# A second X table buffer, generators in two batches, spectra in three slots and a new stage order in a two-branch kernel

## The chip, the cores and the metric

The kernel runs on one core of a Trainium2 chip. The metric is device time in microseconds of one execution, the median of the runs shown; less is better.

## The reference

Two branches of the same 2048 positions by 640 channels stand side by side in the output (2048 by 1280, bf16).

```
A: q, k, v = heads(x @ wqkv)                     # 32 heads of 20
   logits[s, w] = q[s] . k[s - 2 w] * 20**-0.5   # w = 0..7, masked before 0
   out_A = (softmax(logits) @ v[s - 2 w]) @ wo
B: K[d, l] = Re sum_n C dt B exp(dt A l)         # 192 complex terms, l = 0..2047
   out_B = causal convolution of u with K, as FFTs of length 4096, + u * Dskip
```

## The kernel before

Branch B works in five chunks of channels (`NCH`, 192 terms wide in the free dimension, with the 128 channels of a chunk on the partitions). For each chunk `K` is a contraction of two tables over the terms, X (20 exponents) and Y (33 exponents), so that each product of entries is one power of `exp(dt A)`. Generators are the powers at exponents 2**0 to 2**10: `magnitudes` (L234) makes their absolute values on ScalarE, `gens` (L245 to L258) their sines and cosines: a shift and an absolute value on VectorE, two sines on ScalarE and one product on VectorE for each power. Chunk 0's generators go straight into its tables; those of chunk 1 (`gens1`) and of chunks 2 to 4 (`gens2`) go to DRAM (`Gd`, L671) and are loaded by `Tables.load` (L289). `ymag` makes the 16 magnitudes that `yneg` (L315) needs for Y's negative exponents, `ypos` the positive ones, `xtab` X by complex products (`cmul`, L270 to L275) from `Gt` of `weights` or `Xg[:, 6]`; its first product takes `Y[:, 32]`. `kgen` (L345 to L362) contracts both tables with 512 small matmuls a chunk. X, Xg and Y have one buffer each.

The rest of branch B for a chunk: `first_u` and `spread`/`f1` make the first FFT stage of u and K, `f2` the spectra (L410, copied by ScalarE at L414), `swap_halves` a copy of u's spectrum with its halves swapped, `product` (L424, L425) the product of the spectra, `ia` the first inverse stage (L437), stored as `Zd` for chunks 0 to 2 and kept as `Z34` for 3 and 4. Eight pieces `last00` to `last13` (`inverse`, L797) end it: each loads u (`uq`, L804), multiplies it by Dskip (L806), adds it to matmuls with the constant `HB` (L813), copies to `ysb` (L814) and stores (L816); `last0*` also load `zq` from `Zd` (L821). HB takes the space of the tables once the last contraction is done.

Branch A: `proj` makes q, k and v for 5 column tiles each (L473, L474) and stores them; four blocks of 512 positions then run `fetch`, `fetch_v`, `logits` (L522, L526), `av` (L552, L558) and `out_proj` (L571).

The order of the work is not that of the text. Every stage stands in `with at(name)`, which gives its instructions the rank of its name in the list `ORDER` as priority; a planner fills each engine's and queue's instruction stream by these priorities, by dependencies and by free buffers. The streams are fixed after that, and each engine and each queue (SP's, which issues nearly all transfers, POOL's, ScalarE's) goes through its own in order. `pin` adds an order of its own among the activations that need different function tables.

Of the kernel before, what the change touches and what calls it, by code (L numbers as in the profile page):

```python
# [147 lines left out]
def partB_prep(tc, pools, prm, Gd):  # L148
# [53 lines left out]
    def weights():  # L202
# [4 lines left out]
        Gt = pp.tile([128, NCH, 2, CW], bf16, name="Gt")  # L207
        br, bi = flip(4, True), flip(5, True)
        pr = [pp.tile([128, Wd], f32, name=f"pr{q}") for q in range(2)]
        for c0, c1, r in ((0, 1, 0), (1, 0, 1)):  # L210
            for (s, b0), (_, b1) in zip(br, bi):
                V.tensor_tensor(out=pr[0][:, s], in0=b0, in1=cc[:, c0, s], op=A.mult)
                if r == 0:
                    V.tensor_tensor(out=pr[1][:, s], in0=b1, in1=cc[:, c1, s], op=A.mult)
                else:
                    V.scalar_tensor_tensor(out=pr[1][:, s], in0=b1, scalar=-1.0, in1=cc[:, c1, s], op0=A.mult, op1=A.mult)
            p3 = [pr[q][:].rearrange("p (c n) -> p c n", c=NCH) for q in range(2)]
            if r == 0:
                V.tensor_tensor(out=Gt[:, :, 0], in0=p3[0], in1=p3[1], op=A.subtract)
            else:  # L220
                V.tensor_tensor(out=Gt[:, :, 1], in0=p3[1], in1=p3[0], op=A.subtract)
        nc.sync.dma_start(out=Gd[1:, :, 6].rearrange("c p r n -> p c (r n)"), in_=Gt[:, 1:].rearrange("p c r n -> p c (r n)"))
# [7 lines left out]
def magnitudes(tc, pools, ta, am, ca, cb):  # L230

    s = slice(CW * ca, CW * cb)
    for k in K_ORDER:
# [630 lines left out]
```

## Time and profile before

| what | us |
|---|---|
| median of 3 runs | 503.28 (502.35 to 505.78) |
| profiled execution | 505.62 |
| its span, first to last instruction | 503.5 |
| TensorE busy in it | 347.2 |
| VectorE busy | 311.3 |
| ScalarE busy | 265.0 |

The span is what the rows of the trace cover; the 2.1 us around it are not in them. Busy time adds up the instructions of one engine; engines overlap, and idle time counts only where the engine is the one that the end waits for. A window is a stretch of the span for which the busy time of each engine is given, with the mean TensorE clock granted in it (1.00 is 2.4 GHz).

### The profile page before, as it was taken

The numbers are of one execution on the slowest core, as the hardware profiler recorded it, in microseconds if no ns is written. First come the engines' busy times: TensorE is split into PE (matmuls) and PEld (weight loads), VectorE is DVE, ScalarE is ACT, GpSimd is POOL, SyncE is SP. The second block draws the span as 40 slices with busy tenths as digits, with TensorE's granted clock in tenths as the row PEclk, the third lists the DMA queues.
The fourth block names the chain that finished last, engine by engine and source line by source line (L and its number), as shares of the span: only waits on it lengthen the run. The fifth ranks groups of instructions, "written<-read, shape, count | busy, mean of one in ns | idle before, by whom it ended". The sixth has DMA issues, their size and how long they took to land.

```text
span 503.5 us, 13288 instructions
## 1 busy us (share of the span) xinstructions
PE 347.2 (69%) x5684; PEld 215.4 (43%) x5684; DVE 311.3 (62%) x479; ACT 265.0 (53%) x592; POOL 36.4 (7%) x80
## 2 busy tenths in 40 slices
PE   0584298779698728899687596666397788764633
PEld 0232045434246214468444364434165566563422
DVE  0688896599860798987079995189991383021110
ACT  1769866467441164796066652167252587841211
POOL 6820000300000200000020000100000100000000
PEclk9999599599797666899668688599788699775656
DMA  8998684565550577637441029331017650408554
GB/s 251 179 146 182 164 230 155 172 212 204 190 187 5 158 215 203 149 97 206 148 112 23 22 64 279 99 100 23 23 40 199 231 194 33 107 27 226 148 104 70
DMA packets 87562, 70.20 MB, mean 139 GB/s; under 512 B 42864, under 2 KB 79328, under 8 KB 86480
## 3 DMA queue, kind: packets, MB, share of 16 engines
q1 hardware_dynamic: 84096, 63.93, 46.7%
q0 software_dynamic: 2352, 5.18, 3.8%
q8 instruction: 44, 0.72, 0.6%
q10 hardware_dynamic: 1056, 0.25, 0.2%
q14 instruction: 14, 0.11, 0.1%
HBM read 37.35 MB, written 23.63 MB: 121 GB/s over the span
## 4 chain that ended last, share of the span: by engine, by line
PE 34%; DVE 20%; DMA 13%; ACT 10%; issue 8%; SPq 2%; POOL 0%; DVEq 0%; ACTq 0%; POOLq 0%
PE ps_p L473 7%; PE ps_op L571 5%; DVE p L552 4%; PE ps_k L357 4%; PE ps_ia L437 4%; PE ps_k L352 4%; DMA Gdram<-cs 4%; DMA uq<-Udram 3%; DVE krtmp L271 3%; ACT A L396 3%; DVE prod L522 2%; ACT Sp L414 2%; DMA Ytab<-Gdram 2%; PE ps_l L526 2%; DMA qb<-qd 2%
## 5 line engine op out<-in xcount | busy, mean ns | idle before, releaser
L473 PE MATMUL ps_p<-xT,w 128*128 128x512 bf16 x300 | 82.9, 431 | 23.7 <-ACT st L474 18.3
L473 PEld LDWEIGHTS <-w 128*128 128x128 bf16 x300 | 31.1, 107 | 70.2 <-issue 43.6
L522 DVE TENSOR_TENSOR prod<-qb,kb 128x2048 bf16<-128x2048 bf16 x40 | 47.7, 1219 | 15.9 <-DMA kb<-kd 10.9
L558 PE MATMUL ps_o<-p,cHs 64*32 64x256 bf16 x640 | 36.4, 310 | 24.9 <-DVE p L552 23.1
L474 ACT CAST st<-ps_p 128x512 bf16<-128x512 f32 x60 | 34.2, 583 | 34.4 <-PE ps_p L473 32.5
L396 ACT CAST A<-ps_f 128x512 bf16<-128x512 f32 x80 | 42.4, 610 | 18.2 <-PE ps_f L395 18.1
L414 ACT CAST Sp<-ps_f 128x512 bf16<-128x512 f32 (+1 forms) x96 | 42.4, 555 | 16.6 <-PE ps_f L410 16.5
L552 DVE TENSOR_TENSOR p<-vb,attn 128x2048 bf16<-128x2048 bf16 x40 | 48.0, 1218 | 1.9 <-PE ps_o L558 1.8
L357 PE MATMUL ps_k<-Ytab,Xtab 64*20 64x33 bf16 x1280 | 28.0, 244 | 22.8 <-issue 22.8
L410 PE MATMUL ps_f<-A,cT 64*128 64x128 bf16 (+1 forms) x768 | 34.2, 227 | 13.5 <-DMA cT<-k_T 10.3
L270 DVE TENSOR_TENSOR Ytab<-Ytab 128x384 bf16<-128x384 bf16 (+2 forms) x15 | 13.3, 886 | 42.9 <-DMA Ytab<-Gdram 42.8
L410 PEld LDWEIGHTS <-cT 64*128 64x128 bf16 x768 | 27.8, 105 | 26.2 <-issue 14.5
L359 ACT CAST Kd<-ps_k 128x264 bf16<-128x264 f32 x20 | 7.5, 377 | 58.5 <-PE ps_k L357 58.5
L806 DVE TENSOR_TENSOR uq<-uq,Dsb 128x1536 bf16<-128x1536 bf16 (+1 forms) x8 | 6.6, 825 | 46.0 <-DMA uq<-Udram 38.9
L357 PEld LDWEIGHTS <-Xtab 64*20 64x20 bf16 x1280 | 22.4, 123 | 27.1 <-issue 25.0
L558 PEld LDWEIGHTS <-cHs 64*32 64x32 bf16 x640 | 16.0, 99 | 37.1 <-issue 25.4
L814 ACT CAST ysb<-ps_ib 128x384 bf16<-128x384 f32 (+1 forms) x24 | 11.3, 523 | 38.2 <-DMA out_dram<-ysb 25.6
L526 PE MATMUL ps_l<-prod,cGs 128*32 128x512 bf16 x160 | 25.3, 426 | 6.5 <-DVE prod L522 6.4
L571 PE MATMUL ps_op<-wo,oT 128*128 128x320 bf16 x160 | 27.9, 324 | 1.9 <-ACT oT L562 1.9
L352 PE MATMUL ps_k<-Ytab,Xtab 128*20 128x33 bf16 x1280 | 26.9, 249 | 2.4 <-issue 2.4
L424 DVE TENSOR_TENSOR UT<-Sp,UT 128x2048 bf16<-128x2048 bf16 x10 | 11.9, 1220 | 21.8 <-ACT Sp L414 21.8
L438 ACT CAST Z<-ps_ia 128x512 bf16<-128x512 f32 x40 | 20.9, 600 | 8.4 <-PE ps_ia L437 8.2
(108 smaller groups left out, 636.5 us busy)
## 6 DMA issues: line engine op xcount, KB each, us to landing
vb<-vd SPq DMA_DIRECT2D x80, 65.5 KB, 2.3
UT<-Sp SPq DMA_DIRECT2D x10, 512.0 KB, 6.6
HB<-k_HB SPq DMA_DIRECT2D x4, 1024.0 KB, 9.6
Gdram<-cs SPq DMA_DIRECT2D x11, 288.0 KB, 3.6
Zdram<-Z SPq DMA_DIRECT2D x3, 1024.0 KB, 9.2
zq<-Zdram SPq DMA_DIRECT2D x12, 256.0 KB, 4.0
Xg<-Gdram SPq DMA_DIRECT2D x4, 672.0 KB, 6.1
kb<-kd SPq DMA_DIRECT2D x4, 657.5 KB, 8.5
```

Source lines behind the costliest of these rows:

```text
L352: MM(o, lhsT=X[:, :, part, col], rhs=Y[:, :, part, col], start=False, stop=False, tile_position=(0, 32 * g), skip_group_check=True)
L357: MM(o, lhsT=X[hb:hb + 64, :, part - 2, col], rhs=Y[hb:hb + 64, :, part - 2, col], start=False, stop=(part == 3), tile_position=(hb, 32 * ...
L396: nc.scalar.copy(out=A1[:].rearrange("p k r s t -> p (k r) s t")[:, :, sig, 8 * q:8 * q + 8], in_=ps[:])
L410: nc.tensor.matmul(ps[h][:, kk], lhsT=C["T"][hs, k, 64 * (1 - r):64 * (1 - r) + 128], rhs=A1[hs, k, r, s0:s1, :].rearrange("p s t -> p (s ...
L414: nc.scalar.copy(out=o, in_=ps[h][:].rearrange("p k x -> p x k"))
L473: nc.tensor.matmul(ps[:], lhsT=self.w[which][:, kt, 128 * ct:128 * ct + 128], rhs=self.xT[:, kt, 512 * sc:512 * sc + 512], start=(kt == 0) ...
L474: nc.scalar.copy(out=st[:, sc], in_=ps[:])
L522: V.tensor_tensor(out=pr[:], in0=q[:, ct].unsqueeze(1).to_broadcast([128, 4, PB]), in1=windows(k[:, ct, 8 - 8 * wg:8 - 8 * wg + PB], 2, 4) ...
L526: nc.tensor.matmul(ps[mp][r:r + 32], lhsT=C["Gs"][:, ct, :], rhs=pr[:, 2 * mp:2 * mp + 2, PH * half:PH * half + PH], start=(ct == 0), stop ...
L552: V.tensor_tensor(out=p2[:], in0=windows(self.v[b][t][:, 2 * qp:2 * qp + 2, 0:PH], 2, 4), in1=at[:].unsqueeze(2).to_broadcast([128, 4, 2, ...
L558: nc.tensor.matmul(ps[half][32 * q:32 * q + 32, t % 2], lhsT=C["Hs"][r], rhs=p2[r, m, q2, :], start=(t % 2 == 0 and m == 0), stop=(m == 3) ...
L571: nc.tensor.matmul(ps[:], lhsT=oT[:, t, 128 * s:128 * s + 128], rhs=self.wo_sb[:, t, 320 * eh:320 * eh + 320], start=(t == 0), stop=(t == 4))
```

## The change

X gets two buffers (`bufs=2`), and Xg an eighth slot with the generator of 2**7, which `xtab` uses instead of `Y[:, 32]`. Loads of X's and of Y's generators are stages of their own (`tab*`, `taby*`), and so are the magnitudes (`mag*`). Generators are made in two batches, chunks 0 and 1, then 2 to 4; both go through DRAM, the first stored by ScalarE's queue. `cs` gets four buffers. `weights` goes by halves, with `nat` in five buffers. The spectra lie in one tile of three slots: slot 0 for K and the product, 1 and 2 in turn for u. `fetch` loads q and k in ten parts; the products of `logits` and `av` share three buffers. `uq` and `ysb` get two. ORDER is new. The core of the diff:

```diff
-G_SLOTS = [1, 2, 4, 256, 512, 1024, None, 8, 16, 32, 64, 128]
+G_SLOTS = [1, 2, 4, 256, 512, 1024, None, 128, 8, 16, 32, 64]
...
-prep mag0 yneg0 kgen0 q2 mag1 gens1 k3 weights k1 tab1 ypos0 kgen1 u0 q0 q4 xtab1 v2 ypos1 gens0 v1 fetchv0 xtab2 v4 prod0 k4 xtab0 k2 v0
-load kgen4 yneg1 load2 q3 spec swap1 u1 kgen3 spread0 spec0 u v3 prod3 inv0 xtab4 logits0 swap0 inv1 ypos2 fetch1 yneg2 spec1 out1 spread1
-yneg3 inv3 spec2 gens2 hb out0 swap4 k0 av0 swap2 last13 ypos3 swap3 last12 kgen2 xtab3 tab4 fetch2 spread3 tab2 yneg4 ypos4 u2 logits1
-spread2 last03 fetchv1 tab3 fetchv3 last01 av1 last11 q1 logits2 inv2 u3 fetch0 spec3 u4 prod2 last02 prod1 out2 av2 spread4 av3 last00
-fetch3 fetchv2 out3 last10 logits3 inv4 prod4 spec4
+k4 am2 inv4 v0 weights k0 u1 spec2 am0 q3 tab2 tab4 v3 prep load taby2 ypos1 ypos0 out1 xtab2 xtab0 tab1 tab0 q2 q1 swap1 k1 yneg1 load2 v2
+mag2 u0 yneg0 fetch0 v4 q0 spread0 k2 tab3 mag0 kgen2 mag1 gens0 kgen4 last13 q4 fetch1 spec1 inv0 kgen1 kgen0 u2 ypos2 gens2 v1 prod4 taby3
+yneg2 kgen3 k3 taby4 spec3 spec0 taby1 fetch2 ypos3 yneg4 spread3 inv3 logits0 swap0 xtab1 last10 xtab3 u3 inv2 spread1 taby0 u av3 av0
+fetchv0 swap2 last12 av2 out0 prod1 inv1 yneg3 prod2 logits3 spec xtab4 mag4 last03 u4 fetchv1 ypos4 last11 last02 last01 swap3 mag3 out3
+fetchv3 prod3 spec4 fetchv2 spread2 fetch3 av1 swap4 spread4 prod0 last00 out2 logits1 logits2 hb
...
+                pr = [pp.tile([128, 512], f32, name="pr", tag="pr", bufs=2)[:, 0:s.stop - s.start] for _ in range(2)]
+                V.tensor_tensor(out=pr[1], in0=b1, in1=cc[:, c1, s], op=A.mult)
+                    V.tensor_tensor(out=Gt[:, 0, s], in0=pr[0], in1=pr[1], op=A.subtract)
+                    V.scalar_tensor_tensor(out=Gt[:, 1, s], in0=pr[0], scalar=-1.0, in1=pr[1], op0=A.mult, op1=A.subtract)
...
-            cs = gp.tile([128, 4, 2, CW], bf16, name="cs", tag="cs", bufs=2)[:, 0:n]
+        cs = gp.tile([128, 3, 2, CW], bf16, name="cs", tag="cs", bufs=4)[:, 0:n]
+        (nc.sync if ca else nc.scalar).dma_start(out=Gd[ca:cb, :, G_SLOTS.index(2 ** k)].rearrange("c p r n -> p c (r n)"), in_=cs.rearrange("p c r n -> p c (r n)"))
...
-        self.X = tp.tile([128, 20, 2, CW], bf16, name="Xtab", tag="Xtab")
-        self.Xg = tp.tile([128, 7, 2, CW], bf16, name="Xg", tag="Xg")
+        self.X = tp.tile([128, 20, 2, CW], bf16, name="Xtab", tag="Xtab", bufs=2)
+        self.Xg = tp.tile([128, 8, 2, CW], bf16, name="Xg", tag="Xg")
+    def loadx(self, Gd):
+        if self.c:
+            self.nc.sync.dma_start(out=self.Xg[:], in_=Gd[self.c, :, 0:8])
+        else:
+            self.nc.sync.dma_start(out=self.Xg[:, 7:8], in_=Gd[0, :, 7:8])
+            self.nc.sync.dma_start(out=self.Xg[:, 0:6], in_=Gd[0, :, 0:6])
+    def loady(self, Gd):
         for k in range(5):
+            self.nc.sync.dma_start(out=self.Y[:, 16 + 2 ** k], in_=Gd[self.c, :, 8 + k if k < 4 else 7])
...
-        self.mg = [self.pools["prep" if early else "tab"].tile([128, 8, CW], bf16, name="mag", tag="mag", bufs=4 if early else 1) for _ in range(2)]
+        self.mg = [self.pools["tab"].tile([128, 8, CW], bf16, name="mag", tag="mag", bufs=2) for _ in range(2)]
...
-        cmul(nc, X[:, 0:1], Xg[:, 6:7] if w is None else w, self.Y[:, 32], tmp[:, 0:1], True)
+        cmul(nc, X[:, 0:1], Xg[:, 6:7] if w is None else w, Xg[:, 7], tmp[:, 0:1], True)
...
+            o = Sp[:, slots, h, :, 4 * q:4 * q + 4]
+            nc.scalar.copy(out=o, in_=ps[h][:].rearrange("p k (s t) -> p s t k", t=64))
+        nc.vector.tensor_tensor(out=UT[:, h], in0=SK[:, h], in1=UT[:, h], op=A.mult)
+        nc.vector.tensor_tensor(out=SK[:, h], in0=SK[:, h], in1=SU[:, h], op=A.mult)
...
+        for ct in range(5):
+            q = p.tile([128, PB], bf16, name="qb", tag="qb", bufs=3)
+            k = p.tile([128, HALO + PB], bf16, name="kb", tag="kb", bufs=3)
+            nc.sync.dma_start(out=q[:], in_=self.qd[:, ct, i0:i0 + PB])
+            nc.sync.dma_start(out=k[:], in_=self.kd[:, ct, i0:i0 + PB + HALO])
...
-                pr = p.tile([128, 4, PB], bf16, name="prod", tag="prod", bufs=2)
+                pr = p.tile([128, 4, PB], bf16, name="prod", tag="pr", bufs=3)
-                p2 = p.tile([128, 4, 2, PH], bf16, name="p2", tag="p2", bufs=2)
+                p2 = p.tile([128, 4, 2, PH], bf16, name="p2", tag="pr", bufs=3)
...
+    tabs = {}
+        am = pp.tile([128, 11, 3 * CW], bf16, name="am", tag="am")[:, :, 0:(cb - ca) * CW]
+        with at(f"am{ca}"):
+            magnitudes(tc, pools, ta, am, ca, cb)
+        with at(f"gens{ca}"):
+            gens(tc, pools, wi, am, ca, cb, Gd)
+        with at(f"xtab{c}"):
+            tabs[c].xtab(w)
+    batch(0, 2)
+    def table(c, p):
+        tabs[c] = Tables(tc, pools, c)
+        with at(f"tab{c}"):
+            tabs[c].loadx(Gd)
+        with at(f"taby{c}"):
+            tabs[c].loady(Gd)
+        with at(f"mag{c}"):
+            tabs[c].ymag(ta, p)
+    table(0, pin)
+    table(1, pin)
+    batch(2, 5)
+    with at("gens2"):
+        pin(nc.scalar.preload_act_table_set("natural_log_exp_and_others"))
+    Kds[0] = make(0, Gt[:, :, 0:CW].unsqueeze(1))
...
+    Sp = fp.tile([128, 3, 2, 64, 32], bf16, name="Sp")
-        f2(tc, pools, C, A1, SU, 1, 2)
+        f2(tc, pools, C, A1, Sp, 1, 2, slice(1, 2))
...
-            f2(tc, pools, C, A1, Sp, 0, 1 if last else 2)
+            f2(tc, pools, C, A1, Sp, 0, 1 if last else 2, slice(0, 1) if last else slice(0, 3 - c % 2, 2 - c % 2))
-            product(nc, Sp, SU, UT)
+            product(nc, Sp[:, 0], Sp[:, 1 + c % 2], UT)
...
-        uq = ip.tile([128, 6 * 256], bf16, name="uq", tag="uq", bufs=1)[:, 0:512 * n].rearrange("p (x l t) -> p x l t", x=2 * n, l=16)
+        uq = ip.tile([128, 6 * 256], bf16, name="uq", tag="uq", bufs=2)[:, 0:512 * n].rearrange("p (x l t) -> p x l t", x=2 * n, l=16)
-        ysb = ip.tile([128, 16 * 96], bf16, name="ysb", tag="ysb", bufs=1)[:, 0:512 * n].rearrange("p (l x) -> p l x", l=16)
+        ysb = ip.tile([128, 16 * 96], bf16, name="ysb", tag="ysb", bufs=2)[:, 0:512 * n].rearrange("p (l x) -> p l x", l=16)
```

## Rows read from the trace of the kernel before

**Rows 1.** Section 1 of the page, busy us (share of the span) and instructions of each engine

```profile
PE 347.2 (69%) x5684; PEld 215.4 (43%) x5684; DVE 311.3 (62%) x479; ACT 265.0 (53%) x592; POOL 36.4 (7%) x80
```

**Rows 2.** Windows of the whole core: stretch, length, busy us of each engine, TensorE clock, DMA share

```profile
core 0: us, PE busy (x) PEld busy (x) DVE busy (x) ACT busy (x) POOL busy (x), PEclk, DMA share, GB/s
0.00:81.60 81.60, 45.49 (x239) 19.67 (x239) 57.05 (x138) 53.93 (x135) 20.55 (x41) 0.90 0.85 197
...
150.60:165.00 14.40, 12.03 (x514) 9.48 (x509) 1.34 (x1) 1.82 (x5) 0.95 (x3) 0.74 0.06 17
165.00:235.80 70.80, 52.51 (x688) 31.70 (x690) 65.01 (x82) 44.58 (x106) 2.26 (x11) 0.79 0.62 171
235.80:252.00 16.20, 11.53 (x518) 9.51 (x518) 0.29 (x1) 2.42 (x7) 0.19 (x1) 0.72 0.58 159
252.00:305.30 53.30, 41.82 (x508) 24.16 (x507) 49.58 (x68) 34.09 (x77) 2.49 (x6) 0.77 0.26 69
305.30:326.00 20.70, 11.04 (x516) 9.54 (x516) 5.97 (x5) 2.40 (x6) 0.45 (x2) 0.64 0.64 180
326.00:379.60 53.60, 36.25 (x502) 21.63 (x500) 49.49 (x68) 31.04 (x68) 2.21 (x4) 0.88 0.20 51
...
395.30:448.80 53.50, 43.40 (x708) 33.86 (x709) 23.19 (x20) 42.66 (x96) 2.21 (x4) 0.83 0.38 122
448.80:503.50 54.70, 25.55 (x284) 18.75 (x281) 5.64 (x7) 12.03 (x26) 0.00 (x0) 0.61 0.57 132
```

**Rows 3.** Windows of the instructions that write or read Xtab, VectorE, one stretch

```profile
252.00:305.30 53.30, 15.13 (x31) 0.77 0.26 69
```

**Rows 4.** VectorE timeline: first instruction after a contraction: start, us, [idle before <-releaser]

```profile
166.50 0.36 DVE L270 TENSOR_TENSOR Ytab<-Ytab 128x384 bf16<-128x384 bf16 x1 [14.32 <-DMA Ytab<-Gdram]
...
254.95 0.36 DVE L270 TENSOR_TENSOR Ytab<-Ytab 128x384 bf16<-128x384 bf16 x1 [18.86 <-DMA Ytab<-Gdram]
...
329.36 0.36 DVE L270 TENSOR_TENSOR Ytab<-Ytab 128x384 bf16<-128x384 bf16 x1 [8.72 <-DMA Ytab<-Gdram]
```

**Rows 5.** Waits of the stretch 448.8 to 503.5: us in total, times, longest

```profile
DVE uq L806 <- DMA uq<-Udram: 38.9, 6, 10.3
ACT ysb L814 <- DMA out_dram<-ysb: 25.6, 5, 7.4
...
PE ps_ib L813 <- DMA zq<-Zdram: 4.9, 2, 2.6
```

**Rows 6.** Timeline of the last stretch, TensorE, SP's queue and VectorE

```profile
457.38 2.72 PE L813 MATMUL ps_ib<-zq,HB 128*128 128x96 bf16 x32 [0.62 <-issue]
...
465.36 2.72 PE L813 MATMUL ps_ib<-zq,HB 128*128 128x96 bf16 x32 [2.33 <-DMA zq<-Zdram]
...
473.15 2.74 PE L813 MATMUL ps_ib<-zq,HB 128*128 128x96 bf16 x32 [2.60 <-DMA zq<-Zdram]
...
488.66 1.95 SPq L816 DMA_DIRECT2D out_dram<-ysb  x4
489.29 0.69 DVE L806 TENSOR_TENSOR uq<-uq,Dsb 128x1024 bf16<-128x1024 bf16 x1 [5.12 <-DMA uq<-Udram]
...
494.90 0.69 DVE L806 TENSOR_TENSOR uq<-uq,Dsb 128x1024 bf16<-128x1024 bf16 x1 [4.92 <-DMA uq<-Udram]
```

**Rows 7.** Groups of instructions, shapes apart: xcount, busy us, mean ns of one

```profile
L255 DVE SCALAR_TENSOR_TENSOR ab<-ph 128x576 f32<-128x576 int32 x11 | 8.2, 749 | 0.0
...
L255 DVE SCALAR_TENSOR_TENSOR ab<-ph 128x192 f32<-128x192 int32 x22 | 7.5, 350 | 0.9 <-ACT Xg L256 0.9
```

**Rows 8.** Section 6 of the page, transfers: xcount, KB each, median us from issue to landing

```profile
HB<-k_HB SPq DMA_DIRECT2D x4, 1024.0 KB, 9.6
Gdram<-cs SPq DMA_DIRECT2D x11, 288.0 KB, 3.6
...
Xg<-Gdram SPq DMA_DIRECT2D x4, 672.0 KB, 6.1
```

**Rows 9.** Waits of SP's own queue in the first 165 us

```profile
SPq L671 <- DVE cs L257: 15.0, 8, 4.3
```

More of the change, by code (lines that the diff above doesn't have):

```diff
@@ L153, in partB_prep @@
     Wd = NCH * CW
-    nat = [pp.tile([128, NCH, CW], bf16, name="nat", tag="nat", bufs=6) for _ in range(6)]
+    nat = [pp.tile([128, NCH, CW], bf16, name="nat", tag="nat", bufs=5) for _ in range(6)]
     ldt = pp.tile([128, NCH], bf16, name="ldt")
@@ L206, in weights @@
                 nc.scalar.copy(out=cc[:, i, s], in_=ps)
-        Gt = pp.tile([128, NCH, 2, CW], bf16, name="Gt")
+        Gt = pp.tile([128, 2, Wd], bf16, name="Gt")
         br, bi = flip(4, True), flip(5, True)
-        pr = [pp.tile([128, Wd], f32, name=f"pr{q}") for q in range(2)]
         for c0, c1, r in ((0, 1, 0), (1, 0, 1)):
             for (s, b0), (_, b1) in zip(br, bi):
-                V.tensor_tensor(out=pr[0][:, s], in0=b0, in1=cc[:, c0, s], op=A.mult)
+                pr = [pp.tile([128, 512], f32, name="pr", tag="pr", bufs=2)[:, 0:s.stop - s.start] for _ in range(2)]
+                V.tensor_tensor(out=pr[0], in0=b0, in1=cc[:, c0, s], op=A.mult)
+                V.tensor_tensor(out=pr[1], in0=b1, in1=cc[:, c1, s], op=A.mult)
                 if r == 0:
-                    V.tensor_tensor(out=pr[1][:, s], in0=b1, in1=cc[:, c1, s], op=A.mult)
+                    V.tensor_tensor(out=Gt[:, 0, s], in0=pr[0], in1=pr[1], op=A.subtract)
                 else:
[L216 to L222, printed above, removed]
+                    V.scalar_tensor_tensor(out=Gt[:, 1, s], in0=pr[0], scalar=-1.0, in1=pr[1], op0=A.mult, op1=A.subtract)
+        for r in range(2):
+            nc.sync.dma_start(out=Gd[1:, :, 6, r].rearrange("c p n -> p c n"), in_=Gt[:, r, CW:].rearrange("p (c n) -> p c n", n=CW))
         return Gt
@@ L396, in f1, with f2 @@
         nc.scalar.copy(out=A1[:].rearrange("p k r s t -> p (k r) s t")[:, :, sig, 8 * q:8 * q + 8], in_=ps[:])
-def f2(tc, pools, C, A1, Sp, s0, s1):
+def f2(tc, pools, C, A1, Sp, s0, s1, slots):
     nc = tc.nc
@@ L494, in fetch @@
         i0 = PB * b
-        q = self.q[b] = p.tile([128, 5, PB], bf16, name="qb", tag="qb", bufs=1)
-        k = self.k[b] = p.tile([128, 5, HALO + PB], bf16, name="kb", tag="kb", bufs=1)
-        nc.sync.dma_start(out=q[:], in_=self.qd[:, :, i0:i0 + PB])
-        nc.sync.dma_start(out=k[:], in_=self.kd[:, :, i0:i0 + PB + HALO])
+        self.q[b], self.k[b] = [], []
+        for ct in range(5):
[3 more added lines that the diff above has]
+            nc.sync.dma_start(out=k[:], in_=self.kd[:, ct, i0:i0 + PB + HALO])
+            self.q[b].append(q)
+            self.k[b].append(k)
     def fetch_v(self, b):
@@ L504, in fetch_v @@
         for t in range(5):
-            v = p.tile([128, 4, PH + 6], bf16, name="vb", tag="vb", bufs=6)
+            v = p.tile([128, 4, PH + 6], bf16, name="vb", tag="vb", bufs=5)
             for half in range(2):
@@ L520, in logits @@
             for wg in range(2):
[L521 to L522 removed]
+                pr = p.tile([128, 4, PB], bf16, name="prod", tag="pr", bufs=3)
+                V.tensor_tensor(out=pr[:], in0=q[ct][:].unsqueeze(1).to_broadcast([128, 4, PB]), in1=windows(k[ct][:, 8 - 8 * wg:8 - 8 * wg + PB], 2, 4), op=A.mult)
                 for mp in range(2):
@@ L678, in make @@
             tabs[c].yneg()
-        with at(f"xtab{c}"):
-            tabs[c].xtab(w)
         with at(f"kgen{c}"):
@@ L700 @@
                 a.proj(nm, ct)
-    with at("gens1"):
-        batch(1, 2)
-    with at("gens2"):
-        batch(2, 5)
-        pin(nc.scalar.preload_act_table_set("natural_log_exp_and_others"))
     with at("u"):
@@ L714 @@
             nc.sync.dma_start(out=Ud[:, :, s].rearrange("p x l t -> p x (l t)"), in_=uc[:].rearrange("p x l t -> p x (l t)"))
-    with at("tab1"):
-        t1.load(Gd)
     Kds[1] = make(1)
```

61 lines of the change are left out of this document (10 added, 51 removed).

## The prediction

> **What bounds the kernel now.** I read the busy totals first, then the windows by stage, then what the waiting engine waited for at each border of two stages. The totals name no single bound: TensorE is busy 69% of the span and VectorE 62% [rows 1]. The windows say why. Between 165 and 379.6 us two kinds of stretch take turns [rows 2]. In the three long ones VectorE is busy 65.01 of 70.80, 49.58 of 53.30 and 49.49 of 53.60 us, 92 to 93% each, while TensorE is busy 74, 78 and 68%: VectorE bounds them. Between them stand the contractions of `kgen`, 14.40, 16.20 and 20.70 us (chunks 1, 2 and 3), in which TensorE works and VectorE has 1.34, 0.29 and 5.97 us to do. The timeline of VectorE names the reason: at the end of each it had been idle 14.32, 18.86 and 8.72 us for `Ytab<-Gdram` [rows 4], the next chunk's generators, which may not overwrite Y before the contraction has read it. Everything that VectorE makes of a chunk, X too, comes after that, because X has one buffer and starts from a vector that lies in Y. Making X costs VectorE 15.13 us a chunk [rows 3]. At the end, from 448.8 us, no engine is busy half of the time, and the waits there are 38.9 us of VectorE for `uq<-Udram` and 25.6 us of ScalarE for the stores of `ysb` [rows 5]: one buffer each, so that load, product, matmul, copy and store of one piece follow each other.
>
> So I expect the end to be set by VectorE in the long stretches, by TensorE in the contractions, and by transfers behind single buffers at the end. The sum below is made against the profiled execution, 505.6 us (span 503.5 and 2.1 around it); the median of the runs shown is 503.28, 2.3 lower, and the prediction is given for the median.
>
> **Part 1, X beside the contraction.** With two X buffers, and Y's last generator kept a second time in Xg, X of chunk c+1 needs nothing that the contraction of chunk c holds. Chunks 2, 3 and 4 can be made in the windows of chunks 1, 2 and 3, where VectorE has 13.1, 15.9 and 14.7 us free (length less busy) [rows 2]: nearly the 15.13 us that each costs. The long stretches lose that work, but TensorE's work stays, 52.51, 41.82 and 36.25 us [rows 2], so TensorE is late next in the first two, and in the third it is level with what VectorE keeps (49.49 - 15.13 = 34.4). If the engine that bounds them were packed to 93%, as VectorE is now, they would take 56.5, 45.0 and 39.0 us: 14.3, 8.3 and 14.6 saved, together 37. TensorE has not been that dense in this part of the kernel: its best long stretch is 395.3 to 448.8 with 43.40 of 53.50 us, 81% [rows 2]. At 81% they take 64.8, 51.6 and 44.8: 6.0, 1.7 and 8.8 saved, together 16.5. I take the middle, 27, since both ends rest on neighbouring rows. The contractions themselves I leave as they are. Their busy time is 11.0 to 12.0 us and their length 14.40 beside a DMA share of 0.06 and 20.70 beside 0.64 [rows 2], so other transfers beside them could take 8 us off the three or add about as much; that goes into the range.
>
> **Part 2, the start.** The generators of chunks 0 and 1 go in one batch. Of the kind of VectorE instruction that the rows show, 22 at 350 ns and 11 at 749 ns [rows 7] become 11 at about 550 (an estimate halfway) and 11 at 749, 1.6 us less; two more kinds alike, 5 us less in all. Against that, chunk 0's generators now go through DRAM: a store and a load more, 3.6 and 6.1 us by the nearest rows [rows 8], 9.7 us of delay for the first contraction when nothing covers it. TensorE has projections to cover it with, being busy only 45.49 of the first 81.60 us [rows 2]. These eleven stores are issued by ScalarE. On SP's queue the stores of the batches waited 15.0 us in 8 waits for the product they store [rows 9], 1.9 us each; on ScalarE such a wait stands ahead of its own sines and of the copies that free TensorE's PSUM, at most 11 x 1.9 = 21 us, and nothing where the store is placed behind the next sines, which four `cs` buffers allow. The nearest cover is ScalarE's idle time, 27.7 of 81.60 us [rows 2]. I take 4 us for the waits and 1 us for the uncovered part of the round trip: the start comes out even. Ends: 10 us gained (the 5, and as much of X1 made earlier), 31 lost (21 and 9.7).
>
> The Trainium skill, page "DMA: Bandwidth & Descriptors", section "Issuing engines are not separate DMA queues", has it that transfers started by different engines end on the same 16 DMA engines, so that a second issuer saves only issue time. By it these stores land no sooner, and the start would lose the waits for nothing; the row of SP's queue agrees in so far as its time went into waiting for the product, not into bandwidth.
>
> **Part 3, the end.** Eight pieces remain at 448.8. In `last1*` the products of `uq` start 5.6 us apart (489.29 to 494.90), after 5.12 and 4.92 us of waiting for the load, and the four stores of a piece take SP 1.95 us [rows 6]. With two buffers for `uq` and `ysb` what is left of a piece is its matmuls and SP's issues, about 3 us (an estimate from those rows: 1.95 for the stores, 0.4 for a load, and a margin): 3 to 4 intervals save 2.6 each or more, 10 us. `last0*` is another matter: its matmuls follow each other at 457.38, 465.36 and 473.15, 7.9 us apart, and their last waits are for `zq<-Zdram` [rows 6], which keeps its one buffer. These intervals stay. What can shrink there is their number: a piece that is contracted before `inv4` ends leaves the tail. TensorE and ScalarE have some 10 us free each from 395.3 to 448.8 [rows 2], room for one piece: 8 us. I take 18 for the end, with ends 0 and 34 (three pieces moved and the 10). HB, whose rank becomes the last, has four loads of 9.6 us [rows 8]; it was asked for 50 us ahead, and if it came late, the 8 us would go and up to 10 more.
>
> **Part 4, the rest at nothing.** Three spectrum slots instead of two buffers of two: slot 0 is now one for all chunks, so the copies of the next K spectrum wait for the inverse matmuls of this one. ScalarE's 42.66 us of other work in 53.50 [rows 2] hides that; uncovered it would be one inverse, about 6 us, at the last chunk. Forty small loads of q and k instead of eight add issue time to SP, which has idle time, and let the first product start before all five parts are there: between 3 us lost and 5 gained. `weights` makes the same products in halves.
>
> **Sum.** 27 + 0 + 18 + 0 = 45 us; 505.6 - 45 = 460.6 for a profiled execution, 458.3 for the median. I predict 458.
>
> **Rivals.** (a) TensorE takes the bound over: X is hidden, but the stretches go at 81%, the start loses 10 and the end wins only the 10 of the second buffers: 505.6 - 16.5 + 10 - 10 - 2.3 = 487. For it: TensorE's 68 to 81%. Against it: much of TensorE's idle time there is waiting for VectorE's products. (b) Slower: the start slips. The eleven stores hold ScalarE up for the whole 21 us, and the round trip through DRAM is not covered, 31 us before the first contraction, and since the contractions follow each other through the one Y buffer, all of them slip. With the low gains of (a) elsewhere, 16.5 and 10: 505.6 + 31 - 26.5 - 2.3 = 508. It decides from a slip of 26.5 us on, that is, a first contraction that starts after 108 us instead of 81.6. For it: ScalarE is the engine on which sines, copies and the stores meet. Against it: ScalarE is idle a third of that time. (c) The change doesn't do what it says: the stage order puts VectorE's attention products ahead of X, and X stays behind Y; the end's gain is eaten by HB's late loads: 503.3 - 10 + 8 = 501. For it: only the order decides, and its names are all mixed anew. Against it: in the contraction windows nothing else was ready for VectorE. (d) Better than forecast: packed stretches, 37, and three early pieces of the end, 34, less some loss at the start: 505.6 - 71 + 0 - 2.3 = 432.
>
> **How the numbers follow.** Forecast, 440 to 478: 0.58. (a), 478 to 497: 0.18. (b): 0.12. (c): 0.05. (d), below 440: 0.07. Leaving out (b), the slow half of (c) and the far end of (d) gives 436 to 500 for 8 in 10; the likeliest case's own range is 440 to 478. About 1% is what a measurement of this kernel can tell from no change, 498 to 508 here. Faster by more: 0.58 + 0.18 + 0.07 = 0.83; within 1%: (c) 0.05 and none of the others; slower: (b) 0.12.
>
> **What would show it.** Right: X's VectorE instructions of chunks 2 to 4 lie inside the contractions of chunks 1 to 3, and VectorE's wait for `Ytab<-Gdram` shrinks from 42 us in three to under 15; the long stretches are shorter and TensorE is busy over 80% in them; from the last inverse to the end it is some 35 to 45 us rather than 54.7, with `zq` the longest wait. Wrong: X made outside the contractions; a first contraction after 95 us; ScalarE idle in front of its stores; HB landing after the last inverse; or stretches as long as before with TensorE waiting for something that VectorE does not make.

## The result, and the profile after

| | before | after |
|---|---|---|
| median of 4 runs, us | 504.53 (502.35 to 506.01) | 463.20 (462.11 to 465.34) |
| ratio, 95% interval | | 0.919 (0.914 to 0.924) |
| span of the execution whose trace is read | 503.5 | 468.0 |

The forecast was 458 us, with a range of 436 to 500. The trace of after comes from an execution 4.4 to 7.7 us longer than the timed ones (their spans are 460.3 to 463.6), so 35.5 of the 41.3 us can be traced; that of uq_first, below, is 8 us above its median.

In the rows PE and PEld are TensorE's matmuls and its weight loads, DVE is VectorE, ACT ScalarE, POOL GpSimd; SPq and ACTq are the queues that SP and ScalarE issue transfers from.

The page's busy totals answer [rows 1]:

```profile
PE 341.5 (73%) x5672; PEld 214.7 (46%) x5684; DVE 309.3 (66%) x448; ACT 260.9 (56%) x570; POOL 36.7 (8%) x80
```

Each engine's work is nearly what it was; the gain is overlap. The windows, cut at the borders of the contractions, answer [rows 2]:

```profile
core 0: us, PE busy (x) PEld busy (x) DVE busy (x) ACT busy (x) POOL busy (x), PEclk, DMA share, GB/s
0.00:86.10 86.10, 55.79 (x276) 25.11 (x281) 60.56 (x121) 46.86 (x104) 20.84 (x41) 0.84 0.97 231
86.10:111.70 25.60, 24.89 (x563) 13.93 (x567) 23.35 (x44) 23.22 (x43) 0.00 (x0) 0.93 0.43 142
...
138.50:157.40 18.90, 13.66 (x528) 10.13 (x533) 13.66 (x23) 4.34 (x13) 0.00 (x0) 0.79 0.67 204
157.40:220.30 62.90, 40.76 (x581) 27.13 (x585) 54.46 (x77) 38.34 (x91) 3.18 (x13) 0.74 0.41 103
220.30:238.90 18.60, 11.28 (x517) 9.29 (x517) 2.23 (x4) 2.38 (x6) 0.00 (x0) 0.71 0.60 169
238.90:284.80 45.90, 34.95 (x384) 23.61 (x384) 42.13 (x56) 32.46 (x75) 2.63 (x6) 0.82 0.27 75
284.80:300.90 16.10, 11.28 (x517) 9.32 (x517) 4.18 (x10) 1.42 (x4) 0.00 (x0) 0.75 0.49 134
300.90:341.20 40.30, 36.77 (x492) 21.55 (x492) 35.80 (x37) 28.79 (x59) 2.62 (x6) 0.89 0.36 99
...
360.40:423.00 62.60, 53.77 (x890) 36.99 (x887) 47.16 (x42) 47.27 (x106) 2.17 (x4) 0.91 0.43 128
423.00:468.00 45.00, 27.37 (x352) 20.39 (x350) 5.43 (x7) 16.44 (x37) 0.00 (x0) 0.80 0.74 167
```

The long stretches between contractions are now 62.9, 45.9 and 40.3 us. The first two are still VectorE's (87 and 92% busy); in the third TensorE comes to 91%. Behind the last contraction (chunk 4's; "the fourth" in two expectations below) VectorE has 47.16 us of work where it had 23.19 [rows 2]. As ends of steps:

| end of | before, us | after, us | gained so far |
|---|---|---|---|
| contraction of chunk 0 | 95.3 | 111.7 | -16.4 |
| chunk 1 | 163.4 | 157.4 | 6.0 |
| chunk 2 | 251.7 | 238.9 | 12.8 |
| chunk 3 | 325.4 | 300.9 | 24.5 |
| chunk 4 | 395.3 | 360.4 | 34.9 |
| start of the first inverse piece | 449 | 423 | 26 |
| span | 503.5 | 468.0 | 35.5 |

The contraction of chunk 0 lasts longer than before (25.6 us instead of 13.7): projections' matmuls now stand between its own, and TensorE is busy 24.89 us in it. The stretch behind it is 26.8 us instead of 55.3.

Where VectorE makes X is in the windows of the instructions on Xtab, as [rows 3] (length, VectorE busy, count, clock, DMA share and rate):

```profile
86.10:111.70 25.60, 13.97 (x26) 0.93 0.43 142
...
138.50:157.40 18.90, 10.73 (x19) 0.79 0.67 204
157.40:220.30 62.90, 17.86 (x37) 0.74 0.41 103
220.30:238.90 18.60, 1.19 (x3) 0.71 0.60 169
238.90:284.80 45.90, 10.90 (x22) 0.82 0.27 75
284.80:300.90 16.10, 4.18 (x10) 0.75 0.49 134
```

X of chunk 1 lies in the contraction of chunk 0, and X of chunk 2 in that of chunk 1. X of chunks 3 and 4 is made earlier, most of it in the long stretches *ahead* of the contractions it was to lie beside (1.19 and 4.18 us lie inside). X of chunk 3 starts at 178.47, after 6.04 us of waiting for its load into Xg; X of chunk 4 starts at 238.91, when the contraction of chunk 2 has freed a buffer. So beside these contractions VectorE is idle much as before. Its timeline after the contractions of chunks 2, 3 and 4 answers [rows 4]:

```profile
238.91 0.36 DVE L264 TENSOR_TENSOR Xtab<-Xg 128x384 bf16<-128x384 bf16 x1 [16.34 <-PE ps_k L355]
...
304.69 0.36 DVE L264 TENSOR_TENSOR Ytab<-Ytab 128x384 bf16<-128x384 bf16 x1 [15.61 <-DMA Ytab<-Gdram]
...
360.18 0.96 DVE L796 TENSOR_TENSOR uq<-uq,Dsb 128x1536 bf16<-128x1536 bf16 x1 [19.42 <-DMA uq<-Udram]
```

The waits of the last stretch, 423 to 468 us, answer [rows 5]:

```profile
DVE uq L796 <- DMA uq<-Udram: 17.8, 4, 7.7
ACT ysb L804 <- DMA out_dram<-ysb: 14.5, 5, 6.5
PE ps_ib L803 <- DMA zq<-Zdram: 9.4, 3, 5.2
```

The wait for uq has gone from 38.9 to 17.8 us and that for the stores of ysb from 25.6 to 14.5; the one for zq has grown from 4.9 to 9.4. The timeline there, as [rows 6], TensorE, SP's queue and VectorE in order of time:

```profile
431.80 1.78 PE L803 MATMUL ps_ib<-zq,HB 128*128 128x96 bf16 x32 [2.70 <-DMA zq<-Zdram]
...
439.86 1.52 PE L803 MATMUL ps_ib<-zq,HB 128*128 128x96 bf16 x32 [1.51 <-DMA zq<-Zdram]
...
441.41 1.28 SPq L811 DMA_DIRECT2D zq<-Zdram  x3
...
443.27 10.09 SPq L806 DMA_DIRECT2D out_dram<-ysb  x7
...
447.60 2.72 PE L803 MATMUL ps_ib<-zq,HB 128*128 128x96 bf16 x32 [5.20 <-DMA zq<-Zdram]
...
453.47 0.42 SPq L794 DMA_DIRECT2D uq<-Udram  x1
...
456.83 0.69 DVE L796 TENSOR_TENSOR uq<-uq,Dsb 128x1024 bf16<-128x1024 bf16 x1 [7.72 <-DMA uq<-Udram]
```

The pieces with zq still follow each other 8 us apart: the next zq is asked for at 441.41, when its one buffer is free, and contracted at 447.60. Behind them a load of uq (453.47) stands on SP's queue behind seven stores that take it until 453.36.

### The profile page after: what moved, and what is told of

It reads as the page before. It is cut to its first block, busy times and chain, and to the rows that moved or that the text cites. A ratio compares the mean times of both kernels' runs of the same rounds, so it can differ in the third digit from the quotient of the medians.

```text
span 468.0 us, 13264 instructions
## 1 busy us (share of the span) xinstructions
PE 341.5 (73%) x5672; PEld 214.7 (46%) x5684; DVE 309.3 (66%) x448; ACT 260.9 (56%) x570; POOL 36.7 (8%) x80
## 4 chain that ended last, share of the span: by engine, by line
PE 38%; DVE 20%; DMA 16%; issue 12%; ACT 8%; SPq 4%; ACTq 0%; DVEq 0%; POOL 0%; POOLq 0%
PE ps_p L471 10%; PE ps_k L355 6%; PE ps_k L350 6%; PE ps_ia L435 4%; DVE prod L524 4%; DVE p L554 4%; DMA Gdram<-cs 4%; DMA zq<-Zdram 3%; PE ps_ib L803 3%; SPq L453 3%; DMA kd<-st 2%; DVE krtmp L265 2%; ACT mag L307 2%; ACT Sp L412 2%; DMA Xg<-Gdram 2%
## 5 line engine op out<-in xcount | busy, mean ns | idle before, releaser
L471 PE MATMUL ps_p<-xT,w 128*128 128x512 bf16 x288 | 80.2, 421 | 24.3 <-ACT st L472 15.8
L471 PEld LDWEIGHTS <-w 128*128 128x128 bf16 x300 | 30.1, 105 | 63.0 <-issue 33.9
L472 ACT CAST st<-ps_p 128x512 bf16<-128x512 f32 x60 | 34.2, 585 | 31.7 <-PE ps_p L471 23.3
L408 PE MATMUL ps_f<-A,cT 64*128 64x128 bf16 (+1 forms) x768 | 36.4, 230 | 16.3 <-ACT Sp L412 8.6
L412 ACT CAST Sp<-ps_f 128x512 bf16<-128x512 f32 (+1 forms) x96 | 42.8, 579 | 6.0 <-PE ps_f L408 5.9
L355 PE MATMUL ps_k<-Ytab,Xtab 64*20 64x33 bf16 x1280 | 28.3, 244 | 20.2 <-issue 20.2
L408 PEld LDWEIGHTS <-cT 64*128 64x128 bf16 x768 | 31.0, 105 | 25.5 <-issue 24.7
L560 PE MATMUL ps_o<-p,cHs 64*32 64x256 bf16 x640 | 31.2, 308 | 11.4 <-DVE p L554 10.1
L350 PE MATMUL ps_k<-Ytab,Xtab 128*20 128x33 bf16 x1280 | 28.1, 249 | 5.4 <-issue 5.4
L435 PE MATMUL ps_ia<-cE,Sp 128*128 128x128 bf16 x160 | 23.7, 244 | 9.7 <-DVE Sp L423 9.7
L350 PEld LDWEIGHTS <-Xtab 128*20 128x20 bf16 x1280 | 22.6, 128 | 12.8 <-issue 11.2
L307 ACT ACTIVATE mag<-ta 128x192 bf16<-128x192 f32 x80 | 21.7, 353 | 10.4 <-DVE Ytab L313 10.4
L264 DVE TENSOR_TENSOR Ytab<-Ytab 128x384 bf16<-128x384 bf16 (+2 forms) x15 | 13.3, 888 | 21.4 <-DMA Ytab<-Gdram 21.1
```

The source lines that it names most:

```text
L307: pin(self.nc.scalar.activation(out=self.mg[b // 8][:, b % 8], in_=ta[:, s], func=ACT.Exp, scale=-16.0 * (b + 1)))
L350: MM(o, lhsT=X[:, :, part, col], rhs=Y[:, :, part, col], start=False, stop=False, tile_position=(0, 32 * g), skip_group_check=True)
L355: MM(o, lhsT=X[hb:hb + 64, :, part - 2, col], rhs=Y[hb:hb + 64, :, part - 2, col], start=False, stop=(part == 3), tile_position=(hb, 32 * ...
L408: nc.tensor.matmul(ps[h][:, kk], lhsT=C["T"][hs, k, 64 * (1 - r):64 * (1 - r) + 128], rhs=A1[hs, k, r, s0:s1, :].rearrange("p s t -> p (s ...
L412: nc.scalar.copy(out=o, in_=ps[h][:].rearrange("p k (s t) -> p s t k", t=64))
L435: nc.tensor.matmul(ps[:, i], lhsT=X[:, h, 4 * t:4 * t + 4, :].rearrange("p g k -> p (g k)"), rhs=C["E"][:, n_, :], start=(i == 0 and n_ == ...
```

## The experiments

Each run had its own runs of the kernel before on the same chip; their medians lie between 504.05 and 508.41 us, so runs of different groups are compared by the ratio.

| run | median, us | ratio to before (95% interval) |
|---|---|---|
| changed kernel | 463.2 | 0.919 (0.914 to 0.924) |
| x_one | 498.6 | 0.990 (0.985 to 0.995) |
| x_from_y | 513.9 | 1.014 (1.010 to 1.018) |
| hold | 457.0 | 0.905 (0.900 to 0.909) |
| end_one | 478.6 | 0.950 (0.945 to 0.955) |
| store_sp | 481.2 | 0.953 (0.948 to 0.957) |
| old_order | 482.4 | 0.955 (0.950 to 0.960) |
| new_order_before | 525.8 | 1.040 (1.034 to 1.046) |
| zq_two | 474.0 | 0.941 (0.934 to 0.947) |
| uq_first | 456.7 | 0.899 (0.896 to 0.902) |
| uq_only | 468.0 | 0.924 (0.918 to 0.929) |
| hold_zq | 452.8 | 0.896 (0.891 to 0.902) |
| hold_uq_first | 452.2 | 0.892 (0.888 to 0.897) |

**X's buffer and where X starts.** Run x_one takes the second buffer away:

```diff
-        self.X = tp.tile([128, 20, 2, CW], bf16, name="Xtab", tag="Xtab", bufs=2)
+        self.X = tp.tile([128, 20, 2, CW], bf16, name="Xtab", tag="Xtab", bufs=1)
```

> The changed kernel with one X buffer instead of two; all else, the stage order too, as changed. Theory 1 (the second X buffer carries the gain of the chunk periods): X of a chunk again waits for the contraction before, VectorE gets the 15 us a chunk back in the long stretches, and the time rises from 463 to 480 to 490 us. Theory 2 (the new stage order carries it, by moving one block of attention, some 23 us of VectorE, behind the fourth contraction, where VectorE was idle): the time rises by less than 8 us, to at most 471.

Run x_from_y keeps both buffers but lets the first product take Y's vector again:

```diff
-        cmul(nc, X[:, 0:1], Xg[:, 6:7] if w is None else w, Xg[:, 7], tmp[:, 0:1], True)
+        cmul(nc, X[:, 0:1], Xg[:, 6:7] if w is None else w, self.Y[:, 32], tmp[:, 0:1], True)
```

> The changed kernel, but xtab's first product takes the generator of 2**7 from Y again instead of from Xg; X keeps its two buffers. Theory 1 (the second buffer pays only because X needs nothing that lies in Y): X of a chunk again waits for the load into Y, which waits for the contraction before, so most of the second buffer's gain goes: 485 to 500 us, near the 498.6 of one X buffer. Rival (the buffer alone carries it, the slot in Xg only helps the order): under 470 us. In between, the gain is shared.

Without the second buffer 35 us are lost, more than theory 1 expected. Theory 2 falls: with the same order x_one has 9.27 us of VectorE's work behind its last contraction, not 47.16:

```profile
397.00:446.90 49.90, 34.65 (x508) 29.51 (x506) 9.27 (x8) 36.74 (x80) 2.17 (x4) 0.76 0.33 109
```

With the second buffer, but bound to Y, it is worse: 0.095 of the kernel before, 48 us, and again more than expected. The timeline of VectorE in x_from_y shows the binding, after a contraction that ends at 178.6:

```profile
182.27 0.36 DVE L264 TENSOR_TENSOR Ytab<-Ytab 128x384 bf16<-128x384 bf16 x1 [1.51 <-DMA Ytab<-Gdram]
185.19 0.36 DVE L264 TENSOR_TENSOR Xtab<-Xg,Ytab 128x384 bf16<-128x384 bf16 x1 [2.56 <-DMA Ytab<-Gdram]
```

X starts 6.6 us after the contraction, with the load into Y; in x_one, whose contraction ends at 177.7, it starts at once, since Xg is there:

```profile
177.75 0.36 DVE L264 TENSOR_TENSOR Xtab<-Xg 128x384 bf16<-128x384 bf16 x1 [13.48 <-PE ps_k L355]
```

Neither has any X work inside the contractions of chunks 0 to 3. So the buffer and the eighth slot of Xg count only together.

Run hold asks what the forecast had in mind: X of chunks 2 to 4 may not start before the preceding chunk's contraction has begun. The edit makes the first two products depend on the contraction's first matmul:

```diff
-            MM(ps[:], lhsT=self.pools["zero"], rhs=Y[:, 0:8, 0, 0:NB], start=True, stop=False, skip_group_check=True)
+            z = MM(ps[:], lhsT=self.pools["zero"], rhs=Y[:, 0:8, 0, 0:NB], start=True, stop=False, skip_group_check=True)
+            if q == 0:
+                self.pools["begun"] = z.ins.name
...
+        first = pools.get("begun")
+        tabs[c].hold = lambda i: tc.add_manual_dep(i.ins, first, mybir.DependencyInfo(mybir.DependencyClass.Sync, mybir.DependencyReason.DATA), reason="X beside the contraction before")
```

> The changed kernel, with X of chunks 2, 3 and 4 held back until the first matmul of the contraction of the chunk before. If the place of X beside the contraction is worth what the prediction gave it, VectorE is busy 13 us or more in each of the contractions of chunks 1 to 3 (in the changed kernel 12.2, 2.3 and 4.4), the stretches ahead of the contractions of chunks 2 and 3 lose 10 us or more between them, and the time falls to 445 to 455. Rival: TensorE and the waits for it bound those stretches by now, X made early costs nothing, and the time stays at 460 to 468 or rises, since X then delays Y's products behind the contraction.

The windows of Xtab in hold (contractions of chunks 1 and 2, and the stretch behind each):

```profile
140.40:158.80 18.40, 11.51 (x22) 0.80 0.68 217
158.80:208.40 49.60, 3.84 (x9) 0.80 0.52 131
208.40:225.10 16.70, 12.39 (x24) 0.74 0.47 131
225.10:266.80 41.70, 2.82 (x7) 0.78 0.34 101
```

Now 12.39 us of X lie in a contraction that had 1.19, and the stretch ahead of it shrinks from 62.9 to 49.6 us. The end of chunk 2's contraction comes at 225.1 instead of 238.9. VectorE is busy 15.43, 12.66 and 12.78 us in the contractions of chunks 1 to 3. But behind the last contraction it is 69.3 us to the first inverse piece instead of 62.6, and the median gains 6.2 us, a little less than expected. TensorE works there 58.24 us on 893 matmuls at a mean granted clock of 0.84, in the changed kernel 53.77 us on 890 at 0.91; why the clock is lower isn't shown.

**The end's buffers.** Run end_one:

```diff
-        uq = ip.tile([128, 6 * 256], bf16, name="uq", tag="uq", bufs=2)[:, 0:512 * n].rearrange("p (x l t) -> p x l t", x=2 * n, l=16)
+        uq = ip.tile([128, 6 * 256], bf16, name="uq", tag="uq", bufs=1)[:, 0:512 * n].rearrange("p (x l t) -> p x l t", x=2 * n, l=16)
-        ysb = ip.tile([128, 16 * 96], bf16, name="ysb", tag="ysb", bufs=2)[:, 0:512 * n].rearrange("p (l x) -> p l x", l=16)
+        ysb = ip.tile([128, 16 * 96], bf16, name="ysb", tag="ysb", bufs=1)[:, 0:512 * n].rearrange("p (l x) -> p l x", l=16)
```

> The changed kernel with one buffer each for uq and ysb. By the prediction the second buffers are worth 10 us at the end: 473, with the pieces of last1 again some 6 us apart. Rival: the loads of zq alone set the end, and the time stays within 3 us of 463.

The two buffers are worth 15.4 us; in its trace the last stretch is 56.1 us instead of 45.0, and the matmuls of the four pieces without zq start 7.3, 6.0 and 5.7 us apart again, where the changed kernel has 2.6, 4.9 and 2.6.

**The first stores on SP's queue.** Run store_sp:

```diff
-        (nc.sync if ca else nc.scalar).dma_start(out=Gd[ca:cb, :, G_SLOTS.index(2 ** k)].rearrange("c p r n -> p c (r n)"), in_=cs.rearrange("p c r n -> p c (r n)"))
+        nc.sync.dma_start(out=Gd[ca:cb, :, G_SLOTS.index(2 ** k)].rearrange("c p r n -> p c (r n)"), in_=cs.rearrange("p c r n -> p c (r n)"))
```

> The changed kernel with the eleven stores of the first batch issued by SP instead of ScalarE. If ScalarE pays for these stores (4 us taken in the prediction, 21 at most), the time falls by 2 to 6 us. Rival: the wait moves to SP, where the transposed loads of x stand behind it, and the time rises by as much; or nothing, within 2 us.

It loses 18 us: the rival's direction, at more than its price. Its timeline, SP's queue and ScalarE:

```profile
4.91 31.23 SPq L453 DMA_TRANSPOSE xT<-in_A_x_dram  x20
...
36.25 2.12 SPq L252 DMA_DIRECT2D Gdram<-cs  x4
...
38.75 0.53 ACT L248 ACTIVATE cs<-ph 128x384 bf16<-128x384 int32 x1
```

The same two places in the changed kernel, SP's queue and ScalarE's:

```profile
4.97 34.41 SPq L453 DMA_TRANSPOSE xT<-in_A_x_dram  x20
...
23.61 0.43 ACTq L252 DMA_DIRECT2D Gdram<-cs  x1
```

SP's queue is held by twenty transposes until 36.1 us. On ScalarE's queue the first store leaves at 23.61; behind the transposes it leaves at 36.25, with the four `cs` buffers full until then, and the first contraction starts at 102.0 instead of 86.3.

**The stage order.** Run old_order is the changed kernel with the order of before, its new names placed where that order had the work; new_order_before is the kernel before with the new order, without the names it doesn't know.

```diff
 ORDER = """
-k4 am2 inv4 v0 weights k0 u1 spec2 am0 q3 tab2 tab4 v3 prep load taby2 ypos1 ypos0 out1 xtab2 xtab0 tab1 tab0 q2 q1 swap1 k1 yneg1 load2 v2
+prep mag0 yneg0 kgen0 q2 mag1 am2 k3 weights k1 tab1 taby1 ypos0 kgen1 u0 q0 q4 xtab1 v2 ypos1 am0 gens0 tab0 taby0 v1 fetchv0 xtab2 v4 prod0
...
```

> The changed kernel with the stage order of before (its new stage names put where before did that work: am0, tab0 and taby0 beside gens0, am2 beside mag1, tabyN behind tabN, magN ahead of it). If the gain is the buffers' (theory 1, after the run with one X buffer), most of it stays with the old order: 460 to 478. Rival: the buffers pay only with an order made for them, and the time goes back to 485 or more.

> The kernel before with the new stage order (names that it lacks left out, gens1 behind gens0). Theory 1: the order alone brings nothing, 495 to 515. Rival: the order alone moves attention behind the fourth contraction and brings 10 us or more, 493 or less.

Either half alone does less than both: the buffers in the old order gain 22 us, the new order without the buffers loses 21, together they gain 41. Neither time lies in a range that was expected for it. What the old order costs lies behind the contractions: in old_order the last of them ends at 358.5 (360.4 in the changed kernel), but the stretch behind it takes 70.8 us instead of 62.6, and the last one 51.6 instead of 45.0. VectorE's work in the stretch behind is 42.54 us there, so the buffers alone bring most of the attention that moved. The losses of single removals (35, 15 and 19 us) add up to more than the gain, so they don't split it.

**The second zq buffer, and who queues behind it.** Run zq_two gives zq two buffers of its own:

```diff
-        z = fp.tile([128, 128 * 32], bf16, name="zq", tag="Z")[:, 0:3 * 1024].rearrange("p (c x t) -> p c x t", c=3, t=32)
+        z = ip.tile([128, 3 * 1024], bf16, name="zq", tag="zq", bufs=2)[:].rearrange("p (c x t) -> p c x t", c=3, t=32)
```

> The changed kernel with two buffers for zq, in the space of HB's pool. In the changed kernel the matmuls of last0 follow each other 8.8, 8.1 and 7.7 us apart, each after a wait for zq. If that one buffer sets the end now, the intervals fall to 4 to 6 us and the time by 6 to 11, to 452 to 457. Rival: SP's queue with its stores or the DMA engines (busy share 0.74 there) set it, and the time falls by less than 3.

A miss: 474.0, slower by 11. The loss lies ahead of the last stretch, between the last contraction (ended at 353.6) and the first inverse piece: 74 us instead of 62.6. SP's queue and VectorE in zq_two:

```profile
353.74 3.42 SPq L811 DMA_DIRECT2D zq<-Zdram  x6
357.20 1.15 SPq L794 DMA_DIRECT2D uq<-Udram  x2
358.40 5.34 SPq L785 DMA_DIRECT2D HB<-k_HB  x4
...
365.53 0.96 DVE L796 TENSOR_TENSOR uq<-uq,Dsb 128x1536 bf16<-128x1536 bf16 x1 [3.58 <-DMA uq<-Udram]
```

uq's load went out from 353.64 in the changed kernel, 7 us before its contraction ended. Here it goes out at 357.20, after the contraction and behind six loads of zq; uq is there 11.9 us after the contraction, and the attention products queue behind its product on VectorE: the first starts 12.8 us after the contraction, in the changed kernel 8.0. TensorE's mean granted clock in that stretch is lower too, 0.80 against 0.91 (61.67 us for 920 matmuls, 53.77 for 890), so how much of the 11 us is the wait itself isn't shown. Run uq_first is zq_two with uq's load written ahead:

```diff
-        z = zsrc(q)
         uq = ip.tile([128, 6 * 256], bf16, name="uq", tag="uq", bufs=2)[:, 0:512 * n].rearrange("p (x l t) -> p x l t", x=2 * n, l=16)
         nc.sync.dma_start(out=uq.rearrange("p x l t -> p x (l t)"), in_=Ud[:, 2 * c0:2 * (c0 + n), s].rearrange("p x l t -> p x (l t)"))
+        z = zsrc(q)
```

> The changed kernel with zq in two buffers, as in zq_two, and with the load of uq placed ahead of the three loads of zq in each piece of the inverse. In zq_two six loads of zq went out on SP's queue ahead of two of uq after the last contraction, and VectorE's first product of uq, with the products of attention queued behind it, waited for them (uq landed after 8.2 us, at 365.5, which is 11.9 us after the contraction; 5 us later than without the second zq buffer, counted from the contraction's end). Theory 1 (that queueing is what made zq_two 11 us slower): 456 to 466 us. Rival (the second zq buffer slows by the three 1 MB or so of other transfers beside it, or by another stage order, whatever the place of uq): 470 to 478.

456.7 us. The same view of uq_first, whose last contraction ends at 362.3:

```profile
362.43 2.15 SPq L793 DMA_DIRECT2D uq<-Udram  x2
...
366.72 0.96 DVE L796 TENSOR_TENSOR uq<-uq,Dsb 128x1536 bf16<-128x1536 bf16 x1 [22.16 <-DMA uq<-Udram]
```

With two zq buffers uq's load still leaves only after the contraction, but it leaves first: uq is there 4.4 us after the contraction, and the stretch takes 62.7 us again, at a clock of 0.92. So the place on the queue made zq_two slow, and with that out of the way the two edits gain 0.020 of the kernel before, 10 us, on the changed kernel. Run uq_only has the same two lines exchanged and zq's one buffer:

> The changed kernel with the load of uq ahead of the three loads of zq, and zq in its one buffer. It tells which of the two edits of uq_first (456.7 us) brings the 6.5 us against the changed kernel. If the second zq buffer does: 461 to 465, no difference. If the place of uq does: 455 to 459.

Its 468.0 us lies above both ranges; its ratio, 0.924, within the interval of the changed kernel. But in its trace the loads of zq (350.67) still leave ahead of uq (351.99), as without the edit, so it says nothing of uq's place with one zq buffer.

The last two join hold with zq_two, and with uq_first (the diffs are those above):

> X held back as in the run of that name (457.0), and two zq buffers. If the two gains lie at different places they add up: 446 to 451. Rival: the end is bound by the transfers whatever the buffers, 455 to 458.

> hold_zq (X held back until the contraction before has begun, zq in two buffers; 452.8 us) with the load of uq ahead of the loads of zq. Theory 1 as in uq_first: the loads of zq stood ahead of uq here too, so 3 to 8 us are to be had: 445 to 450. Rival: no difference, 451 to 455, since here the wait for uq lay beside work of ScalarE and TensorE.

The second zq buffer takes hold from 0.905 to 0.896, with intervals that just overlap, between the two ranges expected; uq's place then brings nothing that can be told apart (0.892, intervals overlapping): the rival was right there. In all three runs with hold the stretch behind the last contraction takes 69 to 70 us. At 452 us these two are the fastest versions measured.

## Why the prediction was right or wrong

**Part 1, X beside the contraction: 27 forecast; amount near, in part by luck; route half wrong.** From the end of chunk 1's contraction to that of chunk 4's the traces save 231.9 - 203.0 = 28.9 us. Of the three X that were to lie beside contractions, only chunk 2's does for the most part (10.73 us). The failed step is "can be made in the windows of chunks 1, 2 and 3": the new buffer lets X start earlier than that, and the planner's streams take it as soon as its load has landed. VectorE's work in the three long stretches fell by 164.1 - 132.4 = 31.7 us, of which X is 45.4 - 28.8 = 16.6. The rest is attention's products, 73.8 - 57.1 = 16.7 (other work there grew a little); they now stand behind the last contraction, where VectorE has 24 us more to do. There the stretch grew from 53.5 to 62.6, a cost that my sum didn't have. Without what was only put off, 28.9 - 9.1 = 19.8 us remain: the 27 came near in part by luck. The marks say the same: VectorE's wait for `Ytab<-Gdram` fell from 42.8 to 21.1, not below 15, and TensorE is busy over 80% in one long stretch of three. That the buffer is the condition is shown by x_one and x_from_y; that X beside the contraction is the better place, by hold.

**Part 2, the start: 0 forecast, 6 gained by the end of chunk 1's contraction.** The first contraction starts at 86.3 instead of 81.6, inside the bounds, but X of chunk 1 lies beside it (13.97 us), which I had named only as an upper end. VectorE's saving was as forecast: its three kinds of generator instruction take 37.7 us instead of 42.3, 4.6 less (5 forecast). The term for the stores, a loss of 4, came out in size and not in kind: in the first batch ScalarE's sines wait 3.9 us in 4 waits for a `cs` buffer to land, and the profile shows no wait of ScalarE there for VectorE's product. What I hadn't priced is the other queue: chunk 0's stores come while SP is held by the transposes, and there they cost 18 us (store_sp). The Trainium skill, page "DMA: Bandwidth & Descriptors", section "Issuing engines are not separate DMA queues", has it that transfers from different issuers share the same DMA engines, and the traces agree in so far as ScalarE's queue lands these eleven stores no sooner: 4.4 us after their issue (median), against 2.9 from SP's in store_sp. The saving that it calls usually small is the issue; in this case that issue stood behind 31 us of other issues.

**Part 3, the end: 18 forecast, 9.7 in the trace (54.7 to 45.0).** The 10 of the second buffers was a little small: end_one measures 15, its trace 11 in the last stretch. The 8 us for a piece done early failed: all eight pieces still come from 422.8 us on. HB is no cause: its four loads leave at 360.55, and no engine waits for them. In the stretch where TensorE and ScalarE were to have room, both have more to do (53.77 and 47.27 us), and so has VectorE. That the moved attention block took the room is argued from these rows, not shown. The interval of 7.9 us for zq held (8.1 and 7.7), but zq is not the longest wait, which I had given as a sign of being right: it has 9.4 us, uq 17.8.

**Part 4, at nothing.** It wasn't tried by itself, and neither were two smaller changes that come with it, `vb` in five buffers instead of six and `rc` in one instead of two. ScalarE's copies into the spectra show no new wait on the page of after:

```profile
L412 ACT CAST Sp<-ps_f 128x512 bf16<-128x512 f32 (+1 forms) x96 | 42.8, 579 | 6.0 <-PE ps_f L408 5.9
```

Of 6.0 us of idle time before them 5.9 went to the matmuls that they copy, so a slot still being read cost at most 0.1. VectorE's wait for the loads of k, 10.9 us before, is gone; 8.28 us of it lay inside the contraction of chunk 3.

**The sum.** Traced: 28.9 + 6.0 - 9.1 + 9.7 = 35.5 us; forecast 45, from 505.6. Measured between medians: 41.3. So 458 was 5 us low, by the missing 9 us of the moved attention and the missing early piece, against the start's gain. That it came so near is partly luck, since these errors have both signs.

**The rivals.** (a) came true only in the third long stretch. (b) needed a first contraction after 108 us; it came at 86.3, but store_sp, at 102.0, shows how near that lay. (c) was right in one half, that the order decides where X goes (in old_order 9.08 us of X lie in the contraction of chunk 3, here 4.18), and wrong in that nothing would be left.

## What to carry to other kernels

A second buffer moves work to the earliest place that its other inputs allow, not to the idle window next to it: look for what else ties it (here a vector in Y) and, if the window is the goal, tie its start to the window. Where transfers share an in-order queue, read what stands ahead on it at that moment: here one edit went from a loss of 11 us to a gain with the place of one load, and eleven stores behind other issues cost 18. A stage order fits the buffers it was made for; measure each alone before you credit either.

## What was not expected of the hardware

TensorE pauses inside the contractions with no wait that the profile shows. The page's row of after, with its idle time at the end:

```profile
L355 PE MATMUL ps_k<-Ytab,Xtab 64*20 64x33 bf16 x1280 | 28.3, 244 | 20.2 <-issue 20.2
```

It is 20.2 us in 9 pauses of up to 4.0 us, with 5.4 us in 3 more on the line of the larger matmuls, over five contractions; before, the two rows have 22.8 and 2.4 us. Each contraction of chunks 2 to 4 lasts 16 to 19 us for 11.2 us of matmuls. In x_one the two rows have 0.7 and 7.4 us, and those contractions last 13.3 to 14.8. The longest pause:

```profile
350.08 0.44 PE L355 MATMUL ps_k<-Ytab,Xtab 64*20 64x33 bf16 x14 [3.99 <-issue]
```

The page has a row for a queue that carries instructions (packets, MB, share of the 16 engines):

```profile
q8 instruction: 44, 0.72, 0.7%
```

These are 44 transfers of 16 KB, one for some 258 of TensorE's 11,356 matmuls and weight loads; a contraction has 1,032 of these. Every one of the 12 pauses ends 1.3 to 1.7 us after such a transfer has ended: in the longest it runs from 347.29 to 348.61, and TensorE goes on at 350.08. The same holds for the 15 pauses in the contractions of before and the 8 in x_one. So TensorE seems to wait there for its next instructions. That is read from this constant distance; no run changed the contraction itself, and why the transfers come late, and later in some versions than in others, stays open.
